# Gate logits of a top-1 mixture of experts: from token-major products to expert-major ones in four column tiles

## The chip, the cores and the metric

The kernel runs on one core of one Trainium2 chip. The metric is the device time of one execution in microseconds, the median of several runs. A core has five engines that run their own instruction queues in order: PE (matrix products, with PEld for its weight loads), DVE (vector), ACT (scalar), POOL (general purpose) and SP, which here issues the loads and stores. They wait for each other through semaphores. Products land in PSUM, which DVE and ACT read.

## The reference

Sequence length 2048, width 512, hidden width 1792, eight experts, one expert for each token.

```python
x = A_q
h = x + _A_ref(_layernorm(x, axis=-1), A_k, A_v, A_shift_k, A_ssm_k, A_ssm_D)
h2 = h + _B_ref(_layernorm(h, axis=-1), B_w_gate, B_w1, B_w2)
```

`_A_ref` is a short causal convolution of k, a product with v, a long causal convolution along the sequence for each channel (in the reference by an FFT of twice the length), and a product with q. `_B_ref` computes `logits = xf @ w_gate` (eight per token), takes the largest, and adds `silu(xf @ w1[e]) @ w2[e]` of that expert.

## The kernel before

The 2048 tokens lie as 128 partitions by 16 rows (j); four rows make a unit (u = 0 to 3). The 512 channels are four blocks (c = 0 to 3), and each block is worked in two halves, so that the long convolution has eight **rounds** (i = 0 to 7).

A round's work, by line: taps of the short convolution (L252, L260 on ACT, L264 on POOL), a turn by PE (`turn_kv`, L276, four products of 128x128), product with v (L279), the forward stage (`stage_a`, L292, four products per step, copied out by ACT in L295), DVE's turning in 32x32 squares (L317), the two-sided blocks (`blocks`, L328, 32x32 tiles of PE, result in the PSUM tile `pb`, of which there is one), a copy (L334), two products (L337, L341), the blocks back, and DVE's unturning (L349). The last stage (`last_stage`, L364, eight products of two passes per unit) follows per channel block and unit, then the gate with the normed x (L368), the residual (L371, on POOL for c < 3, on DVE for c = 3), which gives h, the store of h, its statistics (L378) and the logits.

The logits of one (c, u): PE turns h (L276), ACT copies it to `ht` (two buffers), PE multiplies each of the four rows, `ht[:, i, :]` of 128 channels by 128 tokens as the stationary operand, with the 128x8 gate weights `wgc[:, c, :]` as the moving one (L386, result 128 tokens by 8 experts), and DVE adds the 128x32 result to `lacc` (L390 for c = 0, L392 else). After all four blocks, `lacc` holds the logits token-major; the routing begins with its maximum over the experts (L606) and the comparison (L610).

The order of all this is made by a planner: every step has an engine, a cost and a due time (built from constants such as DK, DA, DG, DF and a pace), and the planner picks step by step. Its order is fixed when the kernel is built and holds on PE, ACT, DVE, POOL and in SP's queue. PSUM tiles `pa` (two), `pb` (one) and `pm` (two, used by turns and logits) are handed round in that order.

After the convolution come the routing (L595 to L706, with some keep-warm products on PE, L595) and the experts, eight of them in turn with 112 weight tiles loaded by SP.

Of the kernel before, what the change touches and what calls it, by code (L numbers as in the profile page):

```python
# [131 lines left out]
def kernel(  # L132
# [3 lines left out]
    nc = tc.nc  # L136
# [12 lines left out]
    ident = const("id")  # L149
    lacc = keep.tile([P, NJ, E], F32, name="lacc")  # L150
# [30 lines left out]
    NU, UJ = 4, NJ // 4  # L181
# [7 lines left out]
    wgc = cp.tile([P, ND, E], F32, name="wgc")  # L189
# [193 lines left out]
    def logits(c, u):  # L383
        pl = pt("pm", ("pl", c, u), [P, UJ, E])
        for i in range(UJ):
            nc.tensor.matmul(pl[:, i, :], T["ht", c, u][:, i, :], wgc[:, c, :], start=True, stop=True)  # L386

    def sum_logits(c, u):
        if c == 0:
            nc.vector.tensor_copy(lacc[:, unit(u), :], T["pl", c, u])  # L390
        else:
            nc.vector.tensor_add(lacc[:, unit(u), :], T["pl", c, u], lacc[:, unit(u), :])  # L392
# [49 lines left out]
    DA = (-0.959, -0.52, -1.152)

    DG = (-1.949, -3.352, -10.125, -1.421, -6.959, -3.268, -10.578, -16.173, 3.38, 1.806)


    DF = (0.582, 1.843, -1.255, -6.904, -2.929, 0.069, -6.351, 1.525, -1.216, 3.387, -17.611)
    FO, FS = (-0.882, 1.098, 5.515, 2.501), (-0.061, 1.13, 1.203, 0.805)
    DL = -2.865
    DS = (0.755, 3.231, -2.019)  # L450
    DI = (-4.33, -11.042, -4.496, -3.82, -2.749, 3.741, -3.898, -11.729)
    DT = (-3.131, 0.581)
    BU, B0, F0 = 0.756, -0.219, 0.272
    PACE, ZERO, AHEAD = 5.559, 26.619, 1.636
# [24 lines left out]
    for n in range(ND):  # L479
# [77 lines left out]
        for u in range(NU):  # L557
# [22 lines left out]
            add("PE", 1.1, o + DF[7], logits, c, u, uses=[("ht", c, u), "wgc"], makes=[("pm", ("pl", c, u))])  # L580
            add("DVE", 0.16, o + DF[8], sum_logits, c, u, uses=[("pl", c, u)], makes=[(None, ("lg", c, u))])
# [19 lines left out]
    keep_warm(5, 128)  # L601
# [4 lines left out]
    nc.vector.tensor_reduce(mx, lacc, axis=AX.X, op=ALU.max)  # L606
# [3 lines left out]
    nc.vector.tensor_tensor(eq, lacc.rearrange("p j e -> p e j"), to_e(mx), op=ALU.is_ge)  # L610
# [463 lines left out]
```

## Time and profile before

| | |
|---|---|
| median of three runs | 559.26 us (558.04 to 559.94) |
| profiled execution | 555.02 us |
| its span, first to last instruction | 553.1 us |
| PE busy | 530.4 us, 96% |
| PEld busy (loads lie beside products) | 464.8 us, 84% |
| DVE busy | 405.5 us, 73% |
| ACT, POOL busy | 264.4, 257.7 us |
| granted clock, mean | 0.982 |

The page gives the busy time of each engine over the whole span, which mixes stages with different limits. The views by stretch, by line and in order of time give the same for a part. In a row of the timeline stand the start, the duration, the engine, the line of the kernel, the operation, the tiles (written <- read), shapes and count, and in brackets how long the engine sat idle before it and what ended that. Where one row groups several instructions, the duration is from the first start to the last end.

### The profile page before, as it was taken

The numbers are of one execution on the slowest core, as the hardware profiler recorded it, in microseconds if no ns is written. First come the engines' busy times: TensorE is split into PE (matmuls) and PEld (weight loads), VectorE is DVE, ScalarE is ACT, GpSimd is POOL, SyncE is SP. The second block draws the span as 40 slices with busy tenths as digits, with TensorE's granted clock in tenths as the row PEclk, the third lists the DMA queues.
The fourth block names the chain that finished last, engine by engine and source line by source line (L and its number), as shares of the span: only waits on it lengthen the run. The fifth ranks groups of instructions, "written<-read, shape, count | busy, mean of one in ns | idle before, by whom it ended". The sixth has DMA issues, their size and how long they took to land. (4 is left out here: it accounts for less than half of the span.)

```text
span 553.1 us, 12115 instructions
## 1 busy us (share of the span) xinstructions
PE 530.4 (96%) x4799; PEld 464.8 (84%) x4799; DVE 405.5 (73%) x562; ACT 264.4 (48%) x409; POOL 257.7 (47%) x293
## 2 busy tenths in 40 slices
PE   8989989999999889899999999999999999999994
PEld 8956767777768849679999999999998988988973
DVE  3779999978897767876964874884796685694851
ACT  3787877535220326544634544544544553554430
POOL 0275649854660033805901850770680670861731
PEclk9999999999999769999999999999999999999999
DMA  8936686668551259673653556566557467466401
GB/s 290 406 125 215 184 275 179 167 163 284 156 170 40 58 171 343 220 257 144 200 190 127 197 186 198 193 207 214 175 198 261 150 216 256 175 211 220 152 1 41
DMA packets 42452, 105.26 MB, mean 190 GB/s; under 512 B 6464, under 2 KB 14784, under 8 KB 42002
## 3 DMA queue, kind: packets, MB, share of 16 engines
q1 hardware_dynamic: 39602, 95.89, 52.4%
q0 software_dynamic: 2784, 8.51, 4.8%
q8 instruction: 40, 0.66, 0.5%
q14 instruction: 26, 0.21, 0.1%
HBM read 95.96 MB, written 8.47 MB: 189 GB/s over the span
## 5 line engine op out<-in xcount | busy, mean ns | idle before, releaser
L782 DVE TENSOR_TENSOR wlo<-raw,whi 128x1024 fp32r<-128x1024 f32 x112 | 158.9, 1432 | 45.4 <-ACT whi L781 43.6
L801 POOL TENSOR_TENSOR hl<-s,hh 128x240 fp32r<-128x240 f32 (+5 forms) x112 | 114.2, 1033 | 167.2 <-DVE hh L800 166.6
L781 ACT ACTIVATE whi<-raw 128x1024 fp32r<-128x1024 f32 x112 | 114.6, 1052 | 3.6 <-DMA raw<-in_w_dram 3.6
L799 ACT ACTIVATE s<-acc 128x240 f32<-128x240 f32 (+5 forms) x112 | 43.0, 387 | 107.7 <-PE acc L796 66.8
L800 DVE CAST hh<-s 128x240 fp32r<-128x240 f32 (+5 forms) x112 | 56.0, 507 | 37.4 <-ACT s L799 37.2
L796 PE MATMUL acc<-xh,whi 128*128 128x240 f32 (+5 forms) x448 | 72.7, 284 | 0.6 <-ACT xh L757 0.6
L796 PE MATMUL acc<-xl,whi 128*128 128x240 f32 (+5 forms) x448 | 72.0, 283 | 0.0
L796 PE MATMUL acc<-xh,wlo 128*128 128x240 f32 (+5 forms) x448 | 72.0, 283 | 0.0
L796 PEld LDWEIGHTS acc<-xh,whi 128*128 128x128 f32 x448 | 61.7, 189 | 1.3 <-ACT xh L757 0.8
L796 PEld LDWEIGHTS acc<-xl,whi 128*128 128x128 f32 x448 | 61.5, 189 | 0.0
L796 PEld LDWEIGHTS acc<-xh,wlo 128*128 128x128 f32 x448 | 61.4, 189 | 0.0
L816 PE MATMUL acc<-whi,hh 128*128 128x512 f32 (+2 forms) x140 | 55.9, 399 | 0.0
L816 PE MATMUL acc<-whi,hl 128*128 128x512 f32 (+2 forms) x140 | 55.3, 395 | 0.0
L816 PE MATMUL acc<-wlo,hh 128*128 128x512 f32 (+2 forms) x140 | 55.0, 393 | 0.0
L264 POOL TENSOR_TENSOR acc<-acc,ac 128x512 f32<-128x512 f32 x26 | 33.1, 1278 | 37.5 <-ACT ac L260 19.1
L819 PE MATMUL acc<-hh,whi 128*128 128x304 f32 (+2 forms) x168 | 49.8, 296 | 0.0
L819 PE MATMUL acc<-hl,whi 128*128 128x304 f32 (+2 forms) x168 | 49.2, 293 | 0.0
L819 PE MATMUL acc<-hh,wlo 128*128 128x304 f32 (+2 forms) x168 | 49.2, 293 | 0.0
L295 ACT ACTIVATE st<-pa 128x512 f32<-128x512 f32 x64 | 37.1, 595 | 23.3 <-PE pa L292 23.0
L292 PEld LDWEIGHTS pa<-kv,tw 128*128 128x128 f32 x256 | 30.1, 191 | 11.2 <-ACT st L295 6.8
L292 PE MATMUL pa<-kv,tw 128*128 128x128 f32 x256 | 33.1, 281 | 2.9 <-ACT st L295 2.9
L819 PEld LDWEIGHTS acc<-hh,whi 128*128 128x128 f32 x168 | 31.6, 188 | 0.1
(154 smaller groups left out, 874.0 us busy)
## 6 DMA issues: line engine op xcount, KB each, us to landing
raw<-in_w_dram SPq DMA_DIRECT2D x112, 512.0 KB, 4.3
tv<-in_tab_v_dram SPq DMA_DIRECT2D x12, 512.0 KB, 4.3
h<-in_q_dram SPq DMA_DIRECT2D x16, 256.0 KB, 5.0
kt<-in_kt_dram SPq DMA_DIRECT2D x3, 1216.0 KB
kern<-in_ssm_dram SPq DMA_DIRECT2D x12, 256.0 KB, 3.5
v<-in_v_dram SPq DMA_DIRECT2D x12, 256.0 KB
h<-in_x_dram SPq DMA_DIRECT2D x12, 256.0 KB, 2.8
h_dram<-h SPq DMA_DIRECT2D x12, 256.0 KB, 3.9
```

The lines of the kernel that those rows point to most:

```text
L264: nc.gpsimd.tensor_add(T[a, c, u], T[a, c, u], T[b, c, u])
L292: nc.tensor.matmul(p[:, :, j], tw[:, u * UJ + j, r, :], src[:, j, :], start=True, stop=True)
L295: nc.scalar.activation(T["s" + kind, c][:, r * NU + u], T["pa", kind, c, u, r], AF.Copy)
L781: nc.scalar.activation(whi, raw, AF.Copy)
L782: nc.vector.tensor_sub(wlo, raw, whi.bitcast(F32))
L796: nc.tensor.matmul(pu, a[:, k, fs], b[:, k, :], start=i == 0, stop=i == 3 * ND - 1)
L799: nc.scalar.activation(s, pu, AF.Silu)
L800: nc.vector.tensor_copy(hh[:, f, :], s)
L801: nc.gpsimd.tensor_sub(hl[:, f, :], s, hh[:, f, :].bitcast(F32))
L816: nc.tensor.matmul(pd[:ds_.stop - ds_.start], b[:, f, ds_], a[:, f % 2, :], start=f == 0 and i == 0, stop=f == 2 * NCH - 1 and i == 2)
L819: nc.tensor.matmul(pd, a[:, f % 2, ds_], b[:, f, :], start=f == 0 and i == 0, stop=f == 2 * NCH - 1 and i == 2)
```

## The change

The gate's weights become the stationary operand and the turned rows the moving one. For a channel block the weights stand in `wgc` between zeros (24 columns on each side), so that a window of 32 columns puts the eight experts of unit u at rows 8u to 8u+7 and zeros elsewhere. Row j of a unit writes PSUM partitions 32j to 32j+31, its column tile; the second unit of a pair adds into the same accumulator. A pair (two units) makes one 128x128 result, and DVE adds it to `lacc`, now 128x128 with (row, unit, expert) on partitions and tokens along the free side. At the end PE turns `lacc` once into `pl`, from which the maximum and the comparison read. All constants of the planner are new too.

```diff
+    def gate_w(c, u):
+        a = (GAP + E) * c + GAP - E * u
+        return wgc[:, a:a + NU * E]
+
+    def logits(c, p):
+        pl = pt("pm", ("pl", c, p), [P, P])
+        for n, u in enumerate((2 * p, 2 * p + 1)):
+            for j in range(UJ):
+                nc.tensor.matmul(pl[32 * j:32 * j + 32, :], gate_w(c, u), T["ht", c, u][:, j, :],
+                                 start=n == 0, stop=n == 1)
-    def logits(c, u):
-        pl = pt("pm", ("pl", c, u), [P, UJ, E])
-        for i in range(UJ):
-            nc.tensor.matmul(pl[:, i, :], T["ht", c, u][:, i, :], wgc[:, c, :], start=True, stop=True)
...
+        if c == 0 and p == 0:
+            nc.vector.tensor_copy(lacc, T["pl", c, p])
         else:
-            nc.vector.tensor_add(lacc[:, unit(u), :], T["pl", c, u], lacc[:, unit(u), :])
+            nc.vector.tensor_add(lacc, T["pl", c, p], lacc)
...
-    bst1 = cp.tile([P, NJ, 6], F32, name="bst1")
+    bst1 = cp.tile([P, 2, 6], F32, name="bst1")
...
+    nc.gpsimd.memset(wgc, 0.0)
...
-    DK = (-5.802, -1.032, -3.769, -1.022, -0.749, -1.031)
+    DK = (-2.742, -0.93, -7.553, -1.532, -0.994, -6.403)
...
-    PACE, ZERO, AHEAD = 5.559, 26.619, 1.636
+    PACE, ZERO, AHEAD = 5.404, 26.722, 1.943
...
-            add("PE", 1.1, o + DF[7], logits, c, u, uses=[("ht", c, u), "wgc"], makes=[("pm", ("pl", c, u))])
-            add("DVE", 0.16, o + DF[8], sum_logits, c, u, uses=[("pl", c, u)], makes=[(None, ("lg", c, u))])
+            if u % 2:
+                add("PE", 0.75, o + DF[7], logits, c, u // 2, uses=[("ht", c, u - 1), ("ht", c, u), "wgc"],
+                    makes=[("pm", ("pl", c, u // 2))])
+                add("DVE", 0.28, o + DF[8], sum_logits, c, u // 2, uses=[("pl", c, u // 2)] + (["lg"] if c or u > 1 else []),
...
-    keep_warm(5, 128)
...
-    nc.vector.tensor_reduce(mx, lacc, axis=AX.X, op=ALU.max)
+    pl = ps_t.tile([P, P], F32, name="pl", bufs=1)
+    nc.tensor.transpose(pl, lacc, ident)
+    keep_warm(5, 128)
+    four = lambda a: a.rearrange("p (u j) -> p u j", j=4)
+    nc.vector.tensor_reduce(four(mx), pl.rearrange("p (j u e) -> p u j e", u=4, e=E), axis=AX.X, op=ALU.max)
```

The new constants change the order on all engines. Three places follow; line numbers of the changed kernel stand in its rows (L329 for L328, L365 for L364, L293 for L292, L277 for L276, L392 for the logits). First PE in round 4, from the first blocks of the round to its second: before,

```order
L328 MATMUL pb<-xa,cb 32x512 x16
L292 MATMUL pa<-kern,tw 128x128 x4
L276 MATMUL pm<-cs,h 128x128 x4
L292 MATMUL pa<-kv,tw 128x128 x4
L276 MATMUL pm<-cs,acc 128x128 x4
L386 MATMUL pm<-wgc,ht 128x8 x4
L328 MATMUL pb<-xb,cb 32x512 x16
```

and of the changed kernel:

```order
L329 MATMUL pb<-xa,cb 32x512 x16
L365 MATMUL pa<-zs,tv 128x128 x8
L293 MATMUL pa<-kv,tw 128x128 x4
L329 MATMUL pb<-xb,cb 32x512 x16
L293 MATMUL pa<-kv,tw 128x128 x4
```

The logits, both turns and one forward step have left this place, and a last stage has come in. Second, PE at the start of round 6, from the last stage before its first blocks to the one behind its second: before,

```order
L364 MATMUL pa<-zs,tv 128x128 x8
L276 MATMUL pm<-cs,h 128x128 x4
L328 MATMUL pb<-xa,cb 32x512 x16
L386 MATMUL pm<-wgc,ht 128x8 x4
L364 MATMUL pa<-zs,tv 128x128 x8
L328 MATMUL pb<-xb,cb 32x512 x16
```

and of the changed kernel:

```order
L277 MATMUL pm<-cs,h 128x128 x4
L365 MATMUL pa<-zs,tv 128x128 x8
L329 MATMUL pb<-xa,cb 32x512 x16
L392 MATMUL pm<-ht,wgc 32x128 x8
L365 MATMUL pa<-zs,tv 128x128 x8
L329 MATMUL pb<-xb,cb 32x512 x16
```

A pair of units now stands where one unit's logits stood, between first and second blocks. Third, DVE from the last residual (`st<-st`; the last channel block's h lies in a tile named st) to the comparison: before,

```order
L371 TENSOR_TENSOR st<-st 128x512
L392 TENSOR_TENSOR lacc<-pm,lacc 128x32
L396 BN_AGGR rec<-bst_63 128x2 x4
L378 BN_STATS bst_63<-st 128x6 x4
L392 TENSOR_TENSOR lacc<-pm,lacc 128x32
L396 BN_AGGR rec<-bst_63 128x2 x4
L378 BN_STATS bst_63<-st 128x6 x4
L392 TENSOR_TENSOR lacc<-pm,lacc 128x32
L396 BN_AGGR rec<-bst_63 128x2 x4
L392 TENSOR_TENSOR lacc<-pm,lacc 128x32
L606 TENSOR_REDUCE mx<-lacc 128x16
L610 TENSOR_TENSOR eq<-lacc,mx 128x128
```

and of the changed kernel:

```order
L372 TENSOR_TENSOR st<-st 128x512
L399 TENSOR_TENSOR lacc<-pm,lacc 128x128
L403 BN_AGGR rec<-bst_63 128x2 x4
L379 BN_STATS bst_63<-st 128x6 x4
L403 BN_AGGR rec<-bst_63 128x2 x4
L379 BN_STATS bst_63<-st 128x6 x4
L399 TENSOR_TENSOR lacc<-pm,lacc 128x128
L403 BN_AGGR rec<-bst_63 128x2 x4
L621 TENSOR_REDUCE mx<-pl 128x16
L625 TENSOR_TENSOR eq<-pl,mx 128x128
```

Two sums have gone, the last one stands ahead of the last aggregation, and the maximum and the comparison read the turned accumulator.

More of the change, by code (lines that the diff above doesn't have):

```diff
@@ L149 @@
     ident = const("id")
-    lacc = keep.tile([P, NJ, E], F32, name="lacc")
+    lacc = keep.tile([P, P], F32, name="lacc")
     bst2 = keep.tile([P, NJ, ND, 6], F32, name="bst2")
@@ L188 @@
     wg_sb = cp.tile([P, ND, E], F32, name="wg_sb")
-    wgc = cp.tile([P, ND, E], F32, name="wgc")
+    GAP = (NU - 1) * E
+    wgc = cp.tile([P, (GAP + E) * ND + GAP], F32, name="wgc")
     mv1 = cp.tile([P, 2, NJ], F32, name="mv1")
     mva = cp.tile([P, NJ, 2], F32, name="mva")
-    bst1 = cp.tile([P, NJ, 6], F32, name="bst1")
+    bst1 = cp.tile([P, 2, 6], F32, name="bst1")
     quad = [P, UJ, P]
@@ L381, in keep_h, with sum_logits @@
         nc.scalar.activation(sb("ht", ("ht", c, u)), T["pht", c, u], AF.Copy)
-    def logits(c, u):
-        pl = pt("pm", ("pl", c, u), [P, UJ, E])
-        for i in range(UJ):
[L386 to L390, printed above, removed]
+    def gate_w(c, u):
[7 more added lines that the diff above has]
+                                 start=n == 0, stop=n == 1)
+    def sum_logits(c, p):
+        if c == 0 and p == 0:
+            nc.vector.tensor_copy(lacc, T["pl", c, p])
         else:
-            nc.vector.tensor_add(lacc[:, unit(u), :], T["pl", c, u], lacc[:, unit(u), :])
+            nc.vector.tensor_add(lacc, T["pl", c, p], lacc)
     def aggr(u):
@@ L420, in wg_less @@
         for c in range(ND):
-            nc.vector.scalar_tensor_tensor(wgc[:, c, :], T["pc"], -1.0 / D, wg_sb[:, c, :],
+            a = (GAP + E) * c + GAP
+            nc.vector.scalar_tensor_tensor(wgc[:, a:a + E], T["pc"], -1.0 / D, wg_sb[:, c, :],
                                            op0=ALU.mult, op1=ALU.add)
@@ L434 @@
     nc.vector.memset(lacc, 0.0)
-    nc.scalar.activation(mv1[:, 0, 0:1], lacc[:, 0, 0:1], AF.Copy)
+    nc.gpsimd.memset(wgc, 0.0)
+    nc.scalar.activation(mv1[:, 0, 0:1], lacc[:, 0:1], AF.Copy)
     for _ in range(30):
-        nc.tensor.matmul(pt("pa", "warm", [P, P]), lacc.rearrange("p a b -> p (a b)"),
-                         lacc.rearrange("p a b -> p (a b)"), start=True, stop=True)
-    DK = (-5.802, -1.032, -3.769, -1.022, -0.749, -1.031)
[L442 to L453, printed above, removed]
-    PACE, ZERO, AHEAD = 5.559, 26.619, 1.636
+        nc.tensor.matmul(pt("pa", "warm", [P, P]), lacc,
+                         lacc, start=True, stop=True)
+    DK = (-2.742, -0.93, -7.553, -1.532, -0.994, -6.403)
+    DA = (-0.515, -0.166, -1.312)
+    DG = (-7.756, -9.196, -16.731, -2.007, -8.949, -7.899, -12.936, -15.886, 3.939, 2.112)
+    DF = (2.156, 4.2, -1.718, -7.172, -11.095, -0.093, -7.929, 1.515, -6.905, 5.228, -10.922)
+    FO, FS = (-1.91, 0.362, 5.623, -6.9), (1.599, 2.656, 1.572, 1.395)
+    DL = 0.546
+    DS = (0.957, 3.83, -1.763)
+    DI = (-9.018, -15.502, -5.192, -4.441, -8.869, 4.424, -6.64, -17.97)
+    DT = (-3.414, 1.126)
+    BU, B0, F0 = 0.979, -2.491, 0.369
+    PACE, ZERO, AHEAD = 5.404, 26.722, 1.943
     TK = {1: range(0, 3), 2: (), 3: (), 4: range(3, 16)}
@@ L579 @@
             add("ACT", 0.62, o + DF[6], keep_h, c, u, uses=[("pht", c, u)], makes=[("ht", ("ht", c, u))])
[L580 to L581 removed]
+            if u % 2:
+                add("PE", 0.75, o + DF[7], logits, c, u // 2, uses=[("ht", c, u - 1), ("ht", c, u), "wgc"],
+                    makes=[("pm", ("pl", c, u // 2))])
+                add("DVE", 0.28, o + DF[8], sum_logits, c, u // 2, uses=[("pl", c, u // 2)] + (["lg"] if c or u > 1 else []),
+                    **(dict(mods=[]) if c or u > 1 else dict(makes=[(None, "lg")])))
             add("DVE", 0.8, o + DF[9], stats, c, u, uses=[("h", c, u)], makes=[(None, ("bs", c, u))])
@@ L609 @@
     eq = small([E, NJ], "eq")
-    nc.vector.tensor_tensor(eq, lacc.rearrange("p j e -> p e j"), to_e(mx), op=ALU.is_ge)
+    nc.vector.tensor_tensor(eq.rearrange("p e (u j) -> p e u j", j=4), pl.rearrange("p (j u e) -> p e u j", u=4, e=E),
+                            four(mx).unsqueeze(1).to_broadcast([P, E, 4, 4]), op=ALU.is_ge)
     nc.vector.reciprocal(rec[:, :, 1], rec[:, :, 1])
```

4 lines of the change are left out of this document (2 added, 2 removed).

## The prediction

> **What bounds the kernel now.** I first split the span into stages with the view of busy time by stretch: the rounds of the convolution from 87 us on, their tail with the routing's start, and the experts.
>
> ```profile
> 87.00:173.00 86.00, 84.59 (x1275) 61.65 (x1273) 74.46 (x96) 33.71 (x46) 53.17 (x80) 1.00 0.61 176
> 173.00:190.00 17.00, 15.21 (x115) 14.55 (x115) 12.66 (x52) 3.38 (x6) 0.28 (x1) 0.86 0.23 64
> 204.00:546.00 342.00, 337.58 (x2381) 314.93 (x2380) 239.56 (x279) 161.95 (x254) 155.16 (x148) 1.00 0.57 193
> ```
>
> The columns are the stretch, its length, then PE, PEld, DVE, ACT and POOL busy, the granted clock, DMA share and GB/s. The experts (204 to 546) are not touched and need the routing's result, so whatever is won before them moves them as a block. In the rounds PE is busy 84.59 of 86 us, DVE 74.46. The lines that the change replaces, from the view of single lines:
>
> ```profile
> L386 PEld LDWEIGHTS pm<-wgc,ht x128: 186/192/333, 93.2 to 189.1; 128*128 128x128 f32 x128
> L386 PE MATMUL pm<-wgc,ht x128: 170/256/381, 93.2 to 189.2; 128*128 128x8 f32 x128
> L392 DVE TENSOR_TENSOR lacc<-pm,lacc x12: 152/182/192, 142.9 to 189.6; 128x32 f32<-128x32 f32 x12
> ```
>
> Each fp32 product runs as two passes, so 64 products are 128 loads of full 128x128 weights, each for 8 columns. A full PE does not show the end by itself. I next followed the PSUM tile pb, which has one buffer, through DVE's and PE's timeline. A half channel's round goes: two-sided blocks on PE, copy on ACT, blocks, product on DVE, blocks, product, blocks back, and the unturning (L349) which frees pb. The ends of L349 are the rounds' ends; below them stands the last round whole.
>
> ```profile
> 84.76 2.29 DVE L349 STREAM_TRANSPOSE zs<-pb 128x2048 f32<-128x2048 f32 x1
> 102.68 2.30 DVE L349 STREAM_TRANSPOSE zs<-pb 128x2048 f32<-128x2048 f32 x1
> 120.42 2.32 DVE L349 STREAM_TRANSPOSE zs<-pb 128x2048 f32<-128x2048 f32 x1
> 137.92 2.32 DVE L349 STREAM_TRANSPOSE zs<-pb 128x2048 f32<-128x2048 f32 x1 [0.29 <-PE pb L328]
> 154.82 2.28 DVE L349 STREAM_TRANSPOSE zs<-pb 128x2048 f32<-128x2048 f32 x1
> ...
> 157.25 1.14 PE L328 MATMUL pb<-xb,cb 32*32 32x512 f32 x32
> 158.58 1.88 ACT L334 ACTIVATE xb<-pb 128x2048 f32<-128x2048 f32 x1 [7.75 <-PE pb L328]
> 160.72 1.14 PE L328 MATMUL pb<-xa,cb 32*32 32x512 f32 x32
> 162.12 2.29 DVE L337 TENSOR_TENSOR p<-pb,xb 128x2048 f32<-128x2048 f32 x1 [0.44 <-PE pb L328]
> 164.47 1.15 PE L328 MATMUL pb<-xa,cb 32*32 32x512 f32 x32 [0.55 <-DVE p L337]
> 165.98 2.27 DVE L341 TENSOR_TENSOR xb<-pb,xb 128x2048 f32<-128x2048 f32 x1
> 168.46 1.14 PE L328 MATMUL pb<-p,cb 32*32 32x512 f32 x32
> 169.34 1.47 PE L328 MATMUL pb<-xb,cb 32*32 32x512 f32 x32
> 170.84 2.32 DVE L349 STREAM_TRANSPOSE zs<-pb 128x2048 f32<-128x2048 f32 x1 [1.52 <-PE pb L328]
> ```
>
> I number the rounds 0 to 7. Rounds 3 to 7 end at 104.98, 122.74, 140.24, 157.10 and 173.16, and round 2 ended at 87.05: 17.9, 17.8, 17.5, 16.9 and 16.1 us. In round 7 each step starts 0.1 to 0.4 us after the one it needs, so 16.1 is about the floor of this chain. PE's work is thus on the path only where it stands in its queue ahead of blocks that are due. **All five rounds at the floor would save 86.1 - 5 x 16.06 = 5.8 us: the upper bound of what the rounds can give.**
>
> **The products.** Where they stand in the way:
>
> ```profile
> 106.65 1.88 ACT L334 ACTIVATE xa<-pb 128x2048 f32<-128x2048 f32 x1 [0.49 <-PE pb L328]
> 109.15 0.98 PE L386 MATMUL pm<-wgc,ht 128*128 128x8 f32 x8
> 110.06 1.14 PE L328 MATMUL pb<-xb,cb 32*32 32x512 f32 x32
> ...
> 141.37 1.06 PE L386 MATMUL pm<-wgc,ht 128*128 128x8 f32 x8
> 142.29 2.06 PE L364 MATMUL pa<-zs,tv 128*128 128x128 f32 x16
> 144.28 1.14 PE L328 MATMUL pb<-xb,cb 32*32 32x512 f32 x32
> ```
>
> From start to next start a unit's logits hold PE 0.91 to 0.92 us: 0.115 per record, though the record is 0.256 long. The same pace holds for full 128-column work:
>
> ```profile
> 173.22 3.90 PE L364 MATMUL pa<-zs,st 128*128 128x128 f32 x32
> ```
>
> That is 0.122 per record. A pair of units costs 1.84 now. The new pair is 8 products, 16 records of 32 stationary and 128 moving columns, spread over four column tiles. Nothing in the trace has this shape. **Above:** if tiles take turns, 16 x 0.122 = 1.95. **Below:** four records per tile at the full overlap, 4 x 0.122 = 0.49. The nearest rows are the blocks (32x32 tiles, 32 records of 512 columns on 16 tiles): a group lasts 1.14 and the next can start after 169.34 - 168.46 = 0.88, so tiles do overlap there. With two records per tile 1.14 is 0.57 a record, of which 512 columns at full pace are 4 x 0.122 = 0.49; some 0.08 per record is not hidden. For 128 columns that makes 0.122 + 0.08 = 0.20 a record and 4 x 0.20 = 0.8 a pair, an estimate from these rows, and the value I take. Eight pairs then free 8 x (1.84 - 0.8) = 8.3 us of PE's time, which is not what the end gains.
>
> [...]
>
> **The rounds with the new order.** I put the new rows of PE and DVE in place of the old with these durations: blocks 1.07, unturning and products 2.3, last stage (L364) 1.99, four products of the forward stage 0.49, a turn 0.45, gate 0.69, statistics 0.8. Round 4, the order shown above: between its first and second blocks stood a forward step, a turn, a forward step, a turn and a logits unit; the second blocks started at 110.06, 1.5 us after ACT's copy ended (108.53). Now a last stage and one forward step stand there, 2.5 us against the 2.1 that ACT needs: 0.4 late. With the other steps round 4 comes to 16.4, 1.4 less. Round 3 loses its two logits units ahead of blocks and a small DVE step ahead of a turning: 0.8 less. Round 5 has a pair ahead of its first blocks (0.8 + 1.99 against 2.3 of the unturning, 0.5 late) and comes to 16.6, 0.9 less. Round 6 keeps its delay: pair and last stage stand ahead of its second blocks, 2.8 where 2.91 stood (141.37 to 144.28); 0.2 less. Round 7: nothing. Sum 3.3. DVE, at 74.5 of then 82.8 us, is late for some products in this count already (its turnings and statistics stand ahead of the first product in rounds 3 and 5); that is why 8.3 us of PE give 3.3. **I take 3.2**, between 0 (DVE absorbs all) and 5.8. Before 87 us no logits run and PE's order is nearly the same; I take 0, within 1 either way.
>
> **The tail.** Timeline from the last gate to the routing's maximum:
>
> ```profile
> 181.66 0.69 DVE L368 TENSOR_TENSOR st<-pa,st 128x512 f32<-128x512 f32 x1
> 182.39 0.69 DVE L371 TENSOR_TENSOR st<-st 128x512 f32<-128x512 f32 x1
> 183.00 0.18 DVE L392 TENSOR_TENSOR lacc<-pm,lacc 128x32 f32<-128x32 f32 x1
> 183.64 0.81 DVE L378 BATCH_NORM_STATS2 bst<-st 128x6 f32<-128x128 f32 x4
> 184.57 0.63 PE L276 MATMUL pm<-cs,st 128*128 128x128 f32 x4
> 185.30 0.60 ACT L381 ACTIVATE ht<-pm 128x512 f32<-128x512 f32 x1 [1.70 <-PE pm L276]
> 185.95 3.58 PE L386 MATMUL pm<-wgc,ht 128*128 128x8 f32 x16 [0.75 <-ACT ht L381]
> 187.86 0.19 DVE L392 TENSOR_TENSOR lacc<-pm,lacc 128x32 f32<-128x32 f32 x1 [1.66 <-PE pm L386]
> 187.97 0.62 DVE L396 BATCH_NORM_AGGREGATE rec<-bst 128x2 f32<-128x24 f32 x4
> 189.57 0.19 DVE L392 TENSOR_TENSOR lacc<-pm,lacc 128x32 f32<-128x32 f32 x1 [0.98 <-PE pm L386]
> 189.79 0.29 DVE L606 TENSOR_REDUCE mx<-lacc 128x16 f32<-128x128 f32 x1
> ...
> L610 DVE TENSOR_TENSOR eq<-lacc,mx x1: 385/385/385, 190.1 to 190.1; 128x128 f32<-128x128 f32 x1
> ```
>
> DVE ends the last residual at 183.08 and then waits for logits (1.66 and 0.98; PE's last 16 records took 3.58 us at a halved clock). After the change DVE has two sums (128x128 like L610, 0.385 at most), three aggregations of 0.62 and two statistics of 0.83 behind that residual: 0.7 + 1.9 + 1.7 = 4.3, without a wait if the last pair is done by 183.08 + 3.3 = 186.4, when its sum is due. The turn of unit 3 can start at 183.1, its copy ends at 184.5, and the pair ends by 186.1 even at the halved clock (1.6); only tiles in turn at that clock, 3.58 as in the row, would end at 188.1 and give 1.7 back. The added turn of lacc (one product, 0.3, doubled at the halved clock) lies beside the last aggregation of 0.62; without that cover it costs 0.6. The maximum starts at 187.4 instead of 189.8; the later steps read PSUM instead of lacc at the same sizes, 0 to 0.2 more, say 0.1. **I take -2.3.** The keep-warm products are the same and keep their place between the maximum and the count.
>
> **Edits at nothing:** zeroing wgc (POOL, idle at the start), two statistics slots for sixteen (one in-order engine), larger sums (8 x 0.385 against 16 x 0.18, the same DVE time), the changed order of the first loads (half a megabyte moved ahead of the last forward table; no row tells its slack, hence the 1 us above).
>
> **Sum:** -3.2 - 2.3 = -5.5. The profiled execution took 555.02 (span 553.1 and 1.9 around it) and would take 549.5. It lies 4.2 below the median of the runs, 559.26, which I carry over: 553.8.
>
> **Rivals.**
> *The column tiles don't overlap:* a pair costs 1.95. Then rounds 5 and 6 are 1.1 us worse each than in my sum, and round 3 and the pair before the back blocks of round 6 lose 0.6 together; 3.2 becomes 0.4, and the tail gives 1.0 of its 2.3 back (between 0 and 1.7): 559.26 - 0.4 - 1.3 = 557.6. For it: no row of this shape; against: the blocks' 0.88.
> *DVE bounds the rounds:* its waits vanish nowhere, rounds give 0, the tail stays: 559.26 - 2.3 = 557.0. For it: 74.46 of 86 busy; against: DVE waited for PE at most rounds' ends, as the 1.52 at 170.84.
> *Rounds reach the floor:* 559.26 - 5.8 - 2.3 = 551.2.
> *Slower, POOL's queue:* the 16 norms of the last channel block now stand in one run ahead of the norm of c=1's unit 3, whose gate stands on DVE ahead of round 6's first product.
>
> ```profile
> 135.67 1.74 POOL L357 TENSOR_SCALAR xn<-h,mv 128x128 f32<-128x128 f32 x4 [8.07 <-DMA h<-in_x_dram]
> ```
>
> Four such steps hold POOL 7 us, and this row shows an x load that was 8 us late. My round 6 starts at 136.9 and that gate falls due 4.4 later, at 141.3; the load, 2.5 us ahead of before with the rounds, lands at 133 and the norm ends by 134.8: 6.5 us to spare. Past that each us of a late load costs one; from 6.5 + 5.5 = 12.0 us late the kernel is slower. At 15: 559.26 - 5.5 + 8.5 = 562.3.
>
> **Chances.** Forecast (552 to 555.5) 0.64, tiles in turn 0.14, DVE 0.12, floor 0.04, slower 0.06. A measurement tells 0.3% (1.7 us, so 557.6) from no change. Faster: 0.62 of the forecast, 0.04 of the floor, 0.07 of the tiles and 0.08 of DVE, 0.81; same 0.02 + 0.07 + 0.04 = 0.13; slower 0.06. The range runs from the floor, 551.2, to the tiles in turn, 557.6; it leaves out the slow case and the far halves of the rivals, some 0.15.
>
> **What would show it.** The pair's start-to-next-start on PE: 0.8, or 1.95 if tiles take turns. The periods of L349: 17.1, 16.4, 16.6, 16.7, 16.1. From the last residual's end to the maximum: 4.3 instead of 6.7, with no wait of DVE over 0.3. POOL's norms of the last block must end before 133 and DVE must not wait for POOL ahead of round 6's product. The experts' stretch must keep its 342 us. If the part before 87 us moves by more than 1 us, the reordering and not the products did it.

## The result and the profile after

The changed kernel takes 549.44 us (median of 4 runs, 548.32 to 550.84), the kernel before 558.65 (4 runs beside it, 557.15 to 559.94). The ratio is 0.9837, with a 95% interval of 0.9801 to 0.9873: **1.6% faster, 9.2 us between the medians**. The forecast was 553.8, its range 551.2 to 557.6. The sign was right and the time lies 1.8 us below the range. The profiled executions tell another story than the medians: 555.02 before, 549.00 after, a difference of 6.0 where 5.5 was forecast. The profile of before is an unusually quick execution: of 96 further ones beside the later runs four took 555.02 or less, and their median is 558.4. That of after is an ordinary one. Where the other 3 us come from is the main question below.

The stages of the two profiles (us). A round's end is the end of the unturning, the tail runs from round 7's end to the routing's maximum, the routing from there to the first product of the experts:

| stage | before | after | difference | forecast |
|---|---|---|---|---|
| end of round 2 | 87.05 | 87.66 | +0.6 | 0 |
| rounds 3 to 7 | 86.11 | 83.94 | -2.2 | -3.2 |
| tail | 16.63 | 13.46 | -3.2 | -2.3 |
| routing | 16.53 | 16.19 | -0.3 | 0 |
| experts to the end of the span | 346.78 | 345.85 | -0.9 | 0 |

Over all profiles of this study the experts' stretch lies between 345.5 and 348.3; the 0.9 of the last row is inside that spread and not counted as an effect.

Busy time by stretch in the changed kernel, with the columns as in the prediction (stretch, length, PE, PEld, DVE, ACT, POOL, clock, DMA share, GB/s):

```profile
88.00:172.00 84.00, 78.36 (x1272) 52.79 (x1272) 73.90 (x92) 34.36 (x47) 54.57 (x80) 1.00 0.60 180
172.00:185.00 13.00, 11.00 (x115) 9.89 (x114) 11.50 (x45) 2.39 (x4) 0.00 (x0) 0.97 0.28 82
199.00:540.00 341.00, 337.70 (x2381) 314.87 (x2379) 239.95 (x279) 162.21 (x254) 159.17 (x148) 1.00 0.57 193
```

PE is down to 78.4 of 84 us in the rounds, DVE is at 73.9. PE now has 5.6 us to spare there and the weight loads have shrunk from 61.7 to 52.8: neither engine is full, and what is left is the chain. The tail runs at a clock of 0.97 instead of 0.86.

The new products, from the view of one line, and one pair with the row that follows it in PE's timeline:

```profile
L392 PEld LDWEIGHTS pm<-ht,wgc x128: 106/109/110, 94.8 to 183.1; 128*32 128x32 f32 x128
L392 PE MATMUL pm<-ht,wgc x128: 272/273/298, 94.8 to 183.2; 128*32 128x128 f32 x128
...
140.82 0.65 PE L392 MATMUL pm<-ht,wgc 128*32 128x128 f32 x16
141.40 2.08 PE L365 MATMUL pa<-zs,tv 128*128 128x128 f32 x16
```

A record is 0.273 long, and 16 of them take 0.58 from the pair's start to the next start. The tiles overlap. The forecast had 0.8.

DVE's unturnings of rounds 2 to 7 after the change:

```profile
85.36 2.30 DVE L350 STREAM_TRANSPOSE zs<-pb 128x2048 f32<-128x2048 f32 x1
103.87 2.32 DVE L350 STREAM_TRANSPOSE zs<-pb 128x2048 f32<-128x2048 f32 x1
120.61 2.32 DVE L350 STREAM_TRANSPOSE zs<-pb 128x2048 f32<-128x2048 f32 x1 [0.22 <-PE pb L329]
137.36 2.32 DVE L350 STREAM_TRANSPOSE zs<-pb 128x2048 f32<-128x2048 f32 x1 [0.55 <-PE pb L329]
153.58 2.32 DVE L350 STREAM_TRANSPOSE zs<-pb 128x2048 f32<-128x2048 f32 x1
169.28 2.32 DVE L350 STREAM_TRANSPOSE zs<-pb 128x2048 f32<-128x2048 f32 x1 [1.84 <-PE pb L329]
```

The ends give periods of 18.5, 16.7, 16.8, 16.2 and 15.7; the forecast was 17.1, 16.4, 16.6, 16.7 and 16.1. Round 3 is 1.4 too long, round 6 is 0.5 shorter than forecast, and round 7 is shorter than the 16.1 that I had called about the floor.

Round 3 is lost in POOL's queue. Four rows of ACT, POOL and PE there, those between them left out:

```profile
85.31 0.72 ACT L253 ACTIVATE acc<-kt,shw_sb 128x512 f32<-128x512 f32 x1 [2.86 <-DMA kt<-in_kt_dram]
88.02 1.29 POOL L265 TENSOR_TENSOR ac<-ac,ohlo_f 128x512 f32<-128x512 f32 x1 [1.83 <-ACT ohlo_f L261]
90.52 2.50 POOL L372 TENSOR_TENSOR h<-h,xn 128x512 f32<-128x512 f32 x2
91.83 0.66 PE L277 MATMUL pm<-cs,h 128*128 128x128 f32 x4 [1.13 <-POOL h L372]
```

Read upwards: the first turn waits for POOL's residual, the residual stands behind two additions of filter taps (L265), these wait for ACT's taps, and ACT waited 2.86 us for the load of kt.

The end of the tail on DVE, from the last residual on:

```profile
180.83 0.69 DVE L372 TENSOR_TENSOR st<-st 128x512 f32<-128x512 f32 x1
181.44 0.28 DVE L399 TENSOR_TENSOR lacc<-pm,lacc 128x128 f32<-128x128 f32 x1
181.64 0.62 DVE L403 BATCH_NORM_AGGREGATE rec<-bst 128x2 f32<-128x24 f32 x4
182.18 0.81 DVE L379 BATCH_NORM_STATS2 bst<-st 128x6 f32<-128x128 f32 x4
...
184.15 0.27 DVE L399 TENSOR_TENSOR lacc<-pm,lacc 128x128 f32<-128x128 f32 x1
184.34 0.62 DVE L403 BATCH_NORM_AGGREGATE rec<-bst 128x2 f32<-128x24 f32 x4
185.06 0.29 DVE L621 TENSOR_REDUCE mx<-pl 128x16 f32<-128x128 f32 x1
```

No row has a wait. From the residual's end (181.52) to the maximum 3.54 us pass, before 6.71. From round 7's end to that residual's end it is 9.92 in both profiles, so the whole gain of the tail, 3.2, is this piece.

### The profile page after: what moved, and what is told of

Its sections match the earlier page's. It is cut to its first block, busy times and chain, and to the rows that moved or that the text cites. A ratio compares the mean times of both kernels' runs of the same rounds, so it can differ in the third digit from the quotient of the medians.

```text
span 547.1 us, 12112 instructions
## 1 busy us (share of the span) xinstructions
PE 521.2 (95%) x4800; PEld 451.8 (83%) x4800; DVE 404.2 (74%) x554; ACT 264.9 (48%) x409; POOL 262.3 (48%) x294
## 3 DMA queue, kind: packets, MB, share of 16 engines
q1 hardware_dynamic: 39602, 95.89, 52.8%
## 5 line engine op out<-in xcount | busy, mean ns | idle before, releaser
L817 POOL TENSOR_TENSOR hl<-s,hh 128x240 fp32r<-128x240 f32 (+5 forms) x112 | 117.2, 1060 | 162.4 <-DVE hh L816 161.8
L812 PEld LDWEIGHTS acc<-xh,whi 128*128 128x128 f32 x448 | 61.7, 189 | 1.3 <-ACT xh L773 0.8
L265 POOL TENSOR_TENSOR acc<-acc,ac 128x512 f32<-128x512 f32 x26 | 33.1, 1279 | 37.5 <-ACT acc L253 19.1
L296 ACT ACTIVATE st<-pa 128x512 f32<-128x512 f32 x64 | 37.3, 595 | 19.7 <-PE pa L293 19.6
L293 PEld LDWEIGHTS pa<-kv,tw 128*128 128x128 f32 x256 | 30.2, 191 | 12.2 <-ACT st L296 8.7
L293 PE MATMUL pa<-kv,tw 128*128 128x128 f32 x256 | 33.5, 282 | 2.2 <-ACT st L296 2.2
```

The costliest lines, as they stand in the source:

```text
L265: nc.gpsimd.tensor_add(T[a, c, u], T[a, c, u], T[b, c, u])
L293: nc.tensor.matmul(p[:, :, j], tw[:, u * UJ + j, r, :], src[:, j, :], start=True, stop=True)
L296: nc.scalar.activation(T["s" + kind, c][:, r * NU + u], T["pa", kind, c, u, r], AF.Copy)
L812: nc.tensor.matmul(pu, a[:, k, fs], b[:, k, :], start=i == 0, stop=i == 3 * ND - 1)
L817: nc.gpsimd.tensor_sub(hl[:, f, :], s, hh[:, f, :].bitcast(F32))
```

## The experiments

All kernels of one table row were timed beside the kernel before on the same chip. "r2 - r0" is the end of round 2 less that of round 0; a half-clock stretch is a time with a granted clock of 0.50, counted up to 180 us, that is ahead of the last residuals. In steps of 1 us that of "before again" reads 0.56, 0.50, 0.50 and 0.74 from 72 to 76, which makes 3.4 us; in steps of 2 us that of "before, third" (0.96, 0.50 and 0.69 from 148) and the two of "copies first" (0.58 and 0.57 from 148; 0.91, 0.50 and 0.74 from 174) make 3.4 as well.

| kernel | median | ratio to before, 95% | r2 - r0 | rounds 3-7 | tail | half-clock stretches to 180 us |
|---|---|---|---|---|---|---|
| before (first profile) | 559.26 | | 41.38 | 86.11 | 16.63 | none |
| before again | 557.31 | 0.9967 to 1.0022 | 42.97 | 86.26 | 16.64 | 72 to 76 |
| before, third | 557.67 | 0.9959 to 1.0005 | 41.38 | 87.86 | 16.85 | 150 to 153 |
| logits only | 557.59 | 0.9968 to 1.0017 | 42.92 | 88.14 | 14.92 | 73 to 77, 179 to 182 |
| order only | 556.97 | 0.9953 to 1.0016 | 41.56 | 88.79 | 16.58 | 176 to 180 |
| full array | 554.42 | 0.9929 to 0.9977 | 40.90 | 87.50 | 14.21 | none |
| same tile | 549.53 | 0.9801 to 0.9853 | 41.55 | 82.70 | 13.31 | none |
| changed kernel | 549.44 | 0.9801 to 0.9873 | 41.61 | 83.94 | 13.46 | none |
| changed kernel again | 548.55 | 0.9785 to 0.9850 | 41.56 | 83.63 | 13.47 | none |
| residuals first | 549.28 | 0.9808 to 0.9864 | 41.51 | 83.30 | 13.33 | none |
| residuals first, taps later | 551.55 | 0.9825 to 0.9899 | 41.65 | 84.30 | 13.30 | none |
| step moved | 559.41 | 0.9984 to 1.0035 | 41.38 | 87.69 | 16.76 | 150 to 153 |
| copies first | 558.05 | 0.9967 to 1.0031 | 40.87 | 87.99 | 18.11 | 148 to 152, 176 to 179 |
| copies first, again | 557.32 | 0.9942 to 1.0004 | 40.88 | 86.51 | 16.66 | none |
| 128 columns | 553.25 | 0.9889 to 0.9947 | 41.37 | 85.98 | 13.84 | none |
| 128 columns, again | 553.07 | 0.9887 to 0.9943 | 41.39 | 85.95 | 13.84 | none |
| both | 553.41 | 0.9880 to 0.9945 | 41.04 | 86.45 | 13.84 | none |
| both, again | 551.91 | 0.9854 to 0.9930 | 41.02 | 88.03 | 13.84 | none |

### The kernel before, again

Nothing is edited.

> The kernel before, unchanged, for another profiled execution and five more times. Its one profile so far took 555.0 us, about 3.6 less than its median. Theory (the tail): the profile's extra speed lies in the stretch with a starving PE between the last unturning and the first expert product (33.2 us in the profile so far), because how long the clock stays at half varies there; a profile near the median shows 2 to 4 us more in that stretch, and the rounds (86.1 us from the end of round 2 to that of round 7) and the experts (346.8 us to the end of the span) stay within 0.5. Rival (the body): the first 87 us, the rounds or the experts carry the extra 3 us and the tail stays at 33.2.

The theory fell: tail and routing are as before, and the extra time lies ahead of the rounds. The profile took 557.32, its span is 2.3 longer. Round 0 ends 1.1 later: PE's 60 opening products took 10.71 us instead of 9.64, and the first turn stands right behind them. Round 2 takes 1.6 more. PE's timeline in round 2, and the view by stretch at that place:

```profile
69.33 0.66 PE L276 MATMUL pm<-cs,acc 128*128 128x128 f32 x4
72.15 3.65 PE L292 MATMUL pa<-kv,tw 128*128 128x128 f32 x16 [2.17 <-ACT st L295]
75.73 1.14 PE L328 MATMUL pb<-xb,cb 32*32 32x512 f32 x32
...
70.00:72.00 2.00, 0.00 (x0) 0.00 (x0) 2.00 (x3) 2.00 (x3) 1.92 (x2) 1.00 0.99 283
72.00:74.00 2.00, 1.85 (x8) 1.85 (x9) 1.97 (x4) 1.20 (x3) 0.62 (x1) 0.53 0.97 360
74.00:76.00 2.00, 2.00 (x26) 1.84 (x40) 1.53 (x5) 0.76 (x2) 0.00 (x0) 0.62 0.62 187
```

The 16 records took 3.65 us. In the first profile the same records, behind the same wait, took 2.05:

```profile
71.05 2.05 PE L292 MATMUL pa<-kv,tw 128*128 128x128 f32 x16 [2.17 <-ACT st L295]
```

The column to read is the granted clock: 0.53 and 0.62 in the four us behind a wait, 1.6 us dear, in one execution and not in the other.

### The products alone, the order alone

The first kernel has the new logits and the planner's old numbers, the second the old logits and the new numbers:

```diff
-    DK = (-2.742, -0.93, -7.553, -1.532, -0.994, -6.403)
+    DK = (-5.802, -1.032, -3.769, -1.022, -0.749, -1.031)
...
-    PACE, ZERO, AHEAD = 5.404, 26.722, 1.943
+    PACE, ZERO, AHEAD = 5.559, 26.619, 1.636
```

> The new logits (pairs of units, four column tiles, one turn at the end) with the old numbers of the planner. Theory (the products): the gain comes with the shorter products and the shorter tail, whatever the numbers: 550 to 553, pair still 0.58 us from start to start, and the tail 13.5 us from the last unturning to the maximum. Rival (the order): the numbers carry at least half of the gain, and this kernel stays at 555 or more against a before of about 559.

> The old logits (a unit at a time, full array) with the new numbers of the planner. Theory (the products): no gain, 557.5 to 561 beside a before of about 559, since a unit still holds PE for 0.92 us and the last sums still wait for it. Rival (the order): 555 or less.

Neither alone gains anything that can be measured: the first run speaks against the theory of the products, the second against that of the order. The new products without their order bring 1.7 us in the tail and lose 2.0 in the rounds. The planner, with the new costs and the old numbers, puts a forward step and a last stage ahead of blocks in round 4, which then takes 20.2. Its clock fell twice, both times behind waits, of 2.18 us in round 2 and of 2.21 and 2.41 at the end of round 7, though no product of the logits has 8 moving columns here. Round 4 first, then the end of round 7:

```profile
114.52 2.05 PE L293 MATMUL pa<-kv,tw 128*128 128x128 f32 x16
116.41 2.04 PE L365 MATMUL pa<-zs,tv 128*128 128x128 f32 x16
118.38 1.14 PE L329 MATMUL pb<-xb,cb 32*32 32x512 f32 x32
...
172.73 1.15 PE L329 MATMUL pb<-p,cb 32*32 32x512 f32 x32 [2.21 <-DVE xb L342]
177.49 5.50 PE L365 MATMUL pa<-zs,st 128*128 128x128 f32 x32 [2.41 <-DVE zs L350]
```

The new order with the old products has rounds 4 and 5 of 16.4 and 16.3, but rounds 3 and 6 of 19.9 and 19.7, where units of 0.92 us stand ahead of blocks; in round 3 PE also waited 1.35 us for POOL's residual, in a profile in which ACT waited 3.09 for the load of kt. The two parts of the change are worth something only together.

### The pair on the full array, and on one tile at a time

The changed kernel in its own order, with a weight operand of 128 columns that holds the eight in the place of the tile's rows and zeros elsewhere (to make room, four tiles of the routing lie in the weights' tile):

```diff
-    GAP = (NU - 1) * E
+    GAP = P - E
...
-                nc.tensor.matmul(pl[32 * j:32 * j + 32, :], gate_w(c, u), T["ht", c, u][:, j, :],
-                                 start=n == 0, stop=n == 1)
+                nc.tensor.matmul(pl, gate_w(c, u, j), T["ht", c, u][:, j, :],
+                                 start=n == 0 and j == 0, stop=n == 1 and j == UJ - 1)
```

> The changed kernel in its own order, with each product of a pair on the full array: the stationary operand is 128 columns wide, with the eight weight columns where the column tile's rows would be and zeros elsewhere, and all eight products add up in one group. Results and all other steps are the same; the cost of a pair alone changes. Theory (the tiles overlap and that matters): a pair takes 8 x 2 x 0.122 = 1.95 us from start to start instead of 0.58, 11 us more of PE's time over eight pairs; the pairs ahead of blocks in rounds 4 to 6 give 2 to 3.5 back, the last pair in the tail 1 to 1.7: 552.5 to 554.5 beside 549.4 for the change. Rival (the gain is that of fewer and later steps, the tiles don't matter): within 1 us of the change, 548.5 to 550.5.

```profile
119.74 2.05 PE L392 MATMUL pm<-ht,wgc 128*128 128x128 f32 x16
121.63 1.98 PE L365 MATMUL pa<-zs,tv 128*128 128x128 f32 x16
```

A pair takes 1.89 and the kernel 554.42, 5.0 more than the changed one. The two ran on different chips; beside its own before this kernel gains 3.6 and the changed one 9.2, which makes 5.6. The rival of the prediction, tiles in turn, was priced at 3.8 more. Rounds 5 and 6 take 18.0 and 18.2 instead of 16.8 and 16.2, the tail 0.75 more. The overlap of the tiles is worth 5 to 6 us here. Its pairs hold PE as long as the old ones did (2 x 0.92), and still this kernel is faster than the one with the new order and the old products; the reason follows below.

Then the two loops of a pair were exchanged, so that four records in a row go to one tile:

```diff
-        for n, u in enumerate((2 * p, 2 * p + 1)):
-            for j in range(UJ):
+        for j in range(UJ):
+            for n, u in enumerate((2 * p, 2 * p + 1)):
```

> The changed kernel with the two loops of a pair exchanged: both products of a column tile stand next to each other, so that four records in a row go to one tile; the same eight products, the same sums. Theory (PE takes its records in order and only neighbours on different tiles overlap): the pair takes 1.0 to 1.95 us from start to start instead of 0.58, and the kernel 1 to 3 us more. Rival (four records on each of four tiles set the time, whatever their order, 4 x 0.122 and the rest of the pipe): 0.55 to 0.65, and the time within 0.5 of the change.

```profile
138.99 0.70 PE L392 MATMUL pm<-ht,wgc 128*32 128x128 f32 x16
139.62 2.08 PE L365 MATMUL pa<-zs,tv 128*128 128x128 f32 x16
```

0.63, against 0.58 for the same pair: neighbours need not be on different tiles. The rival stands: 4 x 0.122 = 0.49 for the four records of a tile, and about 0.1 for the rest.

### The changed kernel again, and round 3

> The changed kernel once more, for more times and a second profile. Theory (before's offset is the clock's and not the measurement's): a median of 549 to 550, runs within 548 to 552 while those of before reach from 554 to 563, and a profile with clock 1.00 from 70 to 80 whose rounds 3 to 7 take 83.9 within 0.5. Rival (the change's four runs were lucky ones): a median over 551, and a profile with a clock drop in round 2.

The theory held: 548.55, no half-clock stretch ahead of the tail, rounds 3 to 7 within 0.3 of the first profile.

In the next kernel POOL adds the residuals of units 0 and 1 first; the rows of the order on POOL and ACT:

```diff
+L372 TENSOR_TENSOR h<-h,xn 128x512 x2
 L265 TENSOR_TENSOR ac_1112<-ac_1112,ohlo_f 128x512
 L265 TENSOR_TENSOR acc<-acc,ac_1096 128x512
-L372 TENSOR_TENSOR h<-h,xn 128x512 x2
...
-L261 ACTIVATE ohlo_f<-kt,shw_sb 128x512
-L261 ACTIVATE ac_1160<-kt,shw_sb 128x512
 L335 ACTIVATE xb<-pb 128x2048
 L382 ACTIVATE ht<-pm 128x512 x2
+L261 ACTIVATE ohlo_f<-kt,shw_sb 128x512
+L261 ACTIVATE ac_1212<-kt,shw_sb 128x512
```

> The changed kernel; in round 3 POOL adds the residuals of units 0 and 1 ahead of two additions of filter taps, and ACT makes two taps behind the copies of the block result and of the turned units. PE's, DVE's and the load queue's orders are the same. Theory (round 3 was lost to POOL, which waited in its queue for taps whose input came 2.9 us late): the first turn starts at the end of the forward step before it, the wait of 1.13 us on PE goes, round 3 takes 17.1 to 17.5 instead of 18.5, and the kernel 1.0 to 1.4 less than the change: 548.0 to 548.5. Rival (given back): the taps and their additions are late for the turn of the filtered unit in round 4, which then takes 17.5 or more, and the time stays within 0.4 of the change.

PE's wait for the turn went and round 3 took 17.9, not 17.1 to 17.5, since a new wait stood behind it: ACT's copies of the forward stage had slid behind the two taps.

```profile
94.69 2.05 PE L293 MATMUL pa<-kern,tw 128*128 128x128 f32 x16 [0.73 <-ACT st L296]
```

A second try put those taps behind the copies, and one addition behind POOL's next norm:

> The changed kernel with the residuals of units 0 and 1 first on POOL in round 3, as in the experiment before, but with the two taps of ACT now behind the copies of the forward stage and the addition of one of them behind POOL's next norm, since in that experiment PE waited 0.73 and DVE 0.71 for copies behind those taps. Theory (round 3's length is the lateness of one load: 17.2 us where ACT waited 1.2 to 1.3 for it, 18.2 and 18.5 where it waited 2.5 and 2.9): round 3 takes 17.1 to 17.4 however late the load is, rounds 3 to 7 take 82.5 to 82.9, and the median is 0 to 1.2 below that of the change. Rival: the taps are now late for round 4 and it takes 17.3 or more.

Now ACT's third tap waited 1.73 us for POOL, the next copy with it, and PE for the copy; round 3 took 18.9:

```profile
98.47 2.08 PE L365 MATMUL pa<-zs,tv 128*128 128x128 f32 x16 [1.61 <-ACT st L296]
```

In both, a new wait came up along the two queues. What the edits save when the load is late they do not show: ACT waited only 1.24 and 0.73 us for kt in these two profiles. That round 3's length goes with the load of kt is seen in the unedited orders: ACT waited 2.86, 2.52 and 1.30 us for it in the changed kernel, its repetition and the kernel with exchanged loops, and round 3 took 18.5, 18.2 and 17.2. With the wait at 1.30 the rounds take 82.7, which is 3.4 less than before. That is a match in three profiles, not a test.

### What the clock falls behind

Three experiments on the kernel before. First, one forward step of round 2 was put where the changed kernel has it:

```diff
-L292 MATMUL pa<-kern,tw 128x128 x16
+L292 MATMUL pa<-kern,tw 128x128 x12
 L328 MATMUL pb<-xa,cb 32x512 x16
 L276 MATMUL pm<-cs,acc 128x128 x4
+L292 MATMUL pa<-kern,tw 128x128 x4
 L292 MATMUL pa<-kv,tw 128x128 x8
```

> The kernel before with one forward step of round 2 (four products of the forward stage, 16 records... of which the last of the four groups) moved on PE from ahead of the first blocks to behind the turn that follows them, where the changed kernel has it; one load of the same buffer comes three places later on the load queue for it. Theory (a clock that falls behind a wait): in the second profile of before PE waited 2.17 us for ACT at 69.98 to 72.15 and then ran at 0.53 and 0.62 of its clock for 4 us, which cost 1.6 us; the first profile had the same wait and kept its clock. With the step in the wait, 1.2 us of it are left, the profile shows clock 1.00 from 70 to 80, the end of round 2 lies within 0.4 of 41.4 us behind the end of round 0, and the median falls by 0.8 to 1.6 beside before. Rival (the clock falls there for another reason): the clock still falls in 70 to 80, or the median stays within 0.5 of before.

The edit missed its aim: the wait was still 2.02, since ACT's copies came no earlier, and it tells nothing of the wait. But its profile had a half-clock stretch elsewhere, in round 6. Next, the two copies that PE waits for were put ahead of the copy of the block result:

```diff
+L295 ACTIVATE st<-pa 128x512 x2
 L334 ACTIVATE xa<-pb 128x2048
-L295 ACTIVATE st<-pa 128x512 x2
```

> The kernel before; in round 2 ACT copies two results of the forward stage ahead of the copy of the block result instead of behind it. PE's, DVE's, POOL's and the load queue's orders are the same. PE waited 2.17 us there for those two copies. Theory (the wait lets the clock fall): the wait shrinks below 0.7 us, the clock stays at 1.00 from 70 to 80 us in this profile, the end of round 2 lies 41.4 +-0.3 behind that of round 0, and the median is 0.8 to 1.6 below that of before on the same chip. Rival (the clock falls by itself, wherever PE stands): a drop of some 4 us, 1.6 us dear, is seen before 172 us in this profile or in its repetition as it was in two of four profiles of the old order, and the median stays within 0.6 of before.

> The same kernel as the one with the two copies moved ahead, once more, for a second profile and more times; the theories expect the same of it.

> The kernel before, unchanged, for a third profile. Theory (the wait lets the clock fall): end of round 2 either 41.4 behind that of round 0 with the clock at 1.00, or 43.0 with a clock of 0.5 to 0.6 for 4 us behind the wait of 2.17; all other stages as in the two profiles before (rounds 86.1 to 86.3, tail 16.6, experts 346.3 to 346.8), within 0.5. Rival: another stage is longer by over 1 us.

The wait shrank to 0.56 and round 2 was undisturbed in both profiles, but the median did not move beside before (0.9967 to 1.0031 and 0.9942 to 1.0004), and one of the two profiles had two half-clock stretches further on. The third profile of before had one in round 6 as well:

```profile
146.83 1.97 PE L386 MATMUL pm<-wgc,ht 128*128 128x8 f32 x16
149.38 1.74 PE L328 MATMUL pb<-xb,cb 32*32 32x512 f32 x32 [0.58 <-DVE p L337]
151.05 1.11 PE L276 MATMUL pm<-cs,h 128*128 128x128 f32 x4
...
150.00:152.00 2.00, 2.00 (x37) 0.95 (x6) 1.12 (x3) 0.00 (x0) 0.35 (x1) 0.50 0.92 200
152.00:154.00 2.00, 2.00 (x14) 2.00 (x14) 1.47 (x1) 0.60 (x1) 1.16 (x3) 0.69 0.41 92
```

So the wait of round 2 alone is not the cause. In round 6 what stands ahead is a pair of the old products, 1.97 us in which PE is "busy" with records of 8 moving columns, and a wait of 0.58. The stretch of the kernel with the new order and the old products stands behind such a pair too:

```profile
174.13 1.97 PE L386 MATMUL pm<-wgc,ht 128*128 128x8 f32 x16
176.11 5.50 PE L364 MATMUL pa<-zs,st 128*128 128x128 f32 x32
```

(32 full records, 3.90 long in the prediction's row.) Counted over seven profiles with the old products there are six half-clock stretches, five of them behind such pairs. That led to the last experiment: the kernel before with 128 moving columns in each product, eight of which are read (the statistics take two slots for it, as in the change, and POOL zeroes the weights' tile at the start; neither was tried alone).

```diff
-    wgc = cp.tile([P, ND, E], F32, name="wgc")
+    wgc = cp.tile([P, P + (ND - 1) * E], F32, name="wgc")
...
-            nc.tensor.matmul(pl[:, i, :], T["ht", c, u][:, i, :], wgc[:, c, :], start=True, stop=True)
+            nc.tensor.matmul(pl[:, i, :], T["ht", c, u][:, i, :], wgc[:, E * c:E * c + P], start=True, stop=True)
```

> The kernel before with 128 moving columns instead of 8 in each product of the logits: the eight weight columns and 120 others, whose sums nobody reads. The order of every engine is the same; a product's two records were 0.115 us apart each and would be 0.122. Theory (to the clock an array fed with 8 columns is idle): no half-clock stretch behind the pairs of products in rounds 6 and 7 (140 to 155 and 172 to 180 us), where three of six profiles of the old products had one; the wait of 2.17 us in round 2 can still bring one; the median falls by 0.7 to 2 beside before and the mean clock of the runs rises by 0.002 or more. Rival (only waits count, or chance): drops in rounds 6 or 7 as before, the median within 0.6 of before.

> The same kernel with 128 moving columns once more, for a second profile and more times; the theories expect the same of it.

> Both edits on the kernel before: 128 moving columns in the products of the logits, and the two copies moved ahead in round 2, so that the wait of 2.17 us is gone. Theory (both bring the clock down): no half-clock stretch before 172 us, runs of 553 to 556 with a median near the fastest profiles of before (554 to 555.5), the mean clock at 0.982 or more. Rival: drops stay, median 557 or more, mean clock 0.977 to 0.98.

> The same kernel with both edits once more, for a second profile and more times; the theories expect the same of it.

The times and the clock came as the theory expected, and by more: **16 times the columns in these products, in the same order, make the kernel before 0.8% faster** (553.25 and 553.07 beside 558.12; 0.9889 to 0.9947). The median of the runs' mean clocks rises from 0.977 to 0.989, and the two ranges do not meet (all 34 runs of these kernels 0.984 to 0.991, the 20 of before beside them 0.971 to 0.983). No profile has a half-clock stretch ahead of the tail, and the tail itself shrinks from 16.63 to 13.84. PE's last products and the warming products behind them, and the view by stretch there, with 128 columns:

```profile
185.00 2.06 PE L386 MATMUL pm<-wgc,ht 128*128 128x128 f32 x16
187.34 1.58 PE L595 MATMUL warm<-cs 128*128 128x128 f32 x10 [0.28 <-DVE lacc L392]
...
184.00:186.00 2.00, 2.00 (x20) 1.92 (x18) 2.00 (x14) 0.60 (x1) 0.00 (x0) 1.00 0.47 131
186.00:188.00 2.00, 1.72 (x15) 1.50 (x14) 1.75 (x11) 0.66 (x2) 0.58 (x2) 1.00 0.04 8
```

and in the kernel before at the same place:

```profile
182.00:184.00 2.00, 1.25 (x11) 1.02 (x11) 1.97 (x10) 0.60 (x1) 0.00 (x0) 1.00 0.35 99
184.00:186.00 2.00, 1.25 (x12) 1.02 (x11) 1.69 (x12) 0.60 (x1) 0.00 (x0) 0.83 0.47 131
186.00:188.00 2.00, 2.00 (x10) 2.00 (x10) 0.34 (x4) 0.00 (x0) 0.00 (x0) 0.50 0.03 8
```

The last 16 records take 2.06 instead of the 3.58 quoted in the prediction, and DVE no longer waits for them. The wider products cost nothing visible: rounds 3 to 7 take 85.98. The two runs with both edits took 553.41 and 551.91 and their intervals overlap with those of the wide products alone, so the wait of round 2 adds nothing that these runs can tell. (The 88.03 of the last profile is round 3 again: ACT waited 2.59 us for kt, and the round took 19.4.)

Eight half-clock stretches were seen ahead of 180 us. Five stand behind 1.97 us of 8-column products, with a wait of 0.58 behind them in round 6 and none in round 7; the other three stand behind waits of 2.2 to 2.4, and the longest wait ahead of any is 2.41. The same kernel has one in some executions and not in others: of the three profiles of before the first has none, the second one in round 2 and the third one in round 6.

## Why the prediction was right and wrong

**The step that failed is the offset.** "It lies 4.2 below the median of the runs, 559.26, which I carry over": I took the distance between the profiled execution and the median for a property of the measurement that any kernel would keep. It was a property of the kernel. A common execution of before meets a half-clock stretch ahead of the tail (six over seven profiles of the old products; each cost 1.6 us where rows of the same work can be set side by side, 3.65 for 2.05 in round 2 and 5.50 for 3.90 behind round 7); the one profile that I had met none, and its 60 opening products took 9.64 us, where those of before again took 10.71 and those of the changed kernel 10.51. The runs without a profile say the same: the mean clock of that profile is 0.982, the median of the 96 further executions 0.977, and over a span of 555 us the difference is 2.8 us of clock (an estimate) out of the 3.4 by which their median time lies above it. The rest stays open. With the old products widened and PE's order kept, four profiles have no such stretch; and six profiles of kernels with 128 moving columns in the new order have no stretch up to 180 us. So the offset went with the change. Wide products do not rule the stretches out by themselves: the new products with the old numbers met two, behind waits of over 2 us. How much of the quiet clock of the change belongs to its columns and how much to its shorter waits (1.52 instead of 2.17 in round 2) was not separated. Without it the forecast would have been 549.5, and the median is 549.44; that they meet so closely is luck, as the terms below show.

**The size of the profile's own difference was right**, 6.0 against 5.5, but made of terms that were each off and cancel: the rounds gave 1.0 less than forecast, the part before 87 us cost 0.6, the tail gave 0.9 more, and routing and experts, put at nothing, came out 1.2 shorter:

- *The pair* takes 0.58, not 0.8. The estimate hung on 0.08 per record that would not overlap; the overlap is nearly full.
- *The rounds* gave 2.2 instead of 3.2. Rounds 4 and 5 came out as worked out (16.7 and 16.8 for 16.4 and 16.6), 6 and 7 better by 0.5 and 0.4. The mis-sized term is round 3, "0.8 less", which was 0.6 more: the count put PE's and DVE's rows in line and left POOL's queue out, where the residual stands behind additions that wait for a load. I had looked for that mechanism in round 6 and given it a rival of its own; it was there, in round 3, at 1.3 us when the load is late. In the profile in which ACT waited 1.30 for the load, the term is right (17.2). No row shows the 0.49 taken for four products of the forward stage: they are eight records, 0.98 from start to start, so that in round 4 the last stage and the forward step hold PE for 2.91 (107.71 to 110.62) where 2.5 were counted. Round 7 was no floor because PE's blocks in it started 0.15 to 0.26 behind the copy, the product and the unturning that they need; after the change it is 0.05 or 0.06.
- *The tail* gave 3.2 instead of 2.3. The step from the last residual to the maximum took 3.54 instead of 4.3, because I added durations where DVE's rows start 0.53 to 0.72 apart, and the sums take 0.2 from start to start, not 0.385. The row of 3.58 us "at a halved clock" was read rightly as what DVE waited for. What I did not ask is why the clock was halved: with 128 columns in the same products it stays at 1.00 from 184 to 188, where it was 0.83 and 0.50, and widening them alone brings 2.8 of the 3.2. The 0.1 added for later steps that read PSUM stood on no row: the maximum takes 0.29 in both profiles, the comparison 0.29 where it took 0.39.
- *Before 87 us* nothing was expected, and the profiles differ by 0.6, within the bound of 1. Against the second profile of before round 2 ends 2.1 earlier (89.74), against the third 0.15 (87.81).

**The rivals.** Tiles in turn: excluded by the pair, and priced too low (5 to 5.6 measured with the full array, 3.8 worked out). DVE as the bound: excluded, the rounds gave 2.2, and DVE waits for PE ahead of the unturning of round 7 for 1.84. The floor of the rounds: the last round is 15.7, below what I called the floor. The slower case did not come.

**What the 9.2 us are made of.** The clock, taken alone with the old order and wide products: 558.12 to 553.25, 4.9, of which 2.8 lie in the tail. The rest, about 4 from 553.2 to 549.4 (two chips), comes with the shorter pair and its order: the profiles show 2.0 of it in the rounds (85.98 to 83.94) and 0.4 in the tail (13.84 to 13.46); where the remaining 1.4 lie was not found. The new products with the old numbers and the new order with the old products gained nothing of it.

## What to carry over

Products with few moving columns can be dearer than their time on PE, as here (558.12 with 8 columns, 553.25 with 128, in the same order): where PE is otherwise dense, turn the small operand into the weights or pad the moving one, and look at the granted clock behind them, not at PE's busy share. A profiled execution that lies several us off the median is a finding, not an offset: take a second profile and compare the stages before carrying it over to another kernel. A count that lays out two engines' queues must include each queue that a step of theirs waits for, down to the load at its end.

## What was not expected of the hardware

- Sixteen records of 8 columns, 1.97 us, with a wait of 0.58 behind them or none, were followed by half the clock for 3.4 us in some executions, five times over seven profiles; with 128 columns in the same places they were not, in four profiles out of four. What brings the clock down there, and what picks the executions, was not measured.
- Half the clock was seen behind waits alone too: behind the wait of 2.16 to 2.18 us in round 2 it fell in two of six profiles (before again, and the logits alone). The logits alone, without any 8-column product, fell a second time behind waits of 2.21 and 2.41.
- Sixteen records of 32 stationary and 128 moving columns on four column tiles take 0.58 to 0.63 from start to start, whichever order the tiles come in; the same products on the full array take 1.89.
- The load of kt, issued at the same place of the queue, kept ACT waiting 1.30 to 2.86 us in three profiles of the changed order; between these ends round 3 differs by 1.3 us.
